# GpSimd's port-using instructions wait for the VectorE instruction one ahead of the port-using one planned before them

## The chip, the cores and the metric

One core of one Trainium2 chip. The metric is device time in microseconds of the one launch, as a median of runs: 1325.54 us for the kernel before (three runs, 1324.97 to 1326.35).

## The reference, cut to what matters

The input is 2 x 4096 tokens of 192 values. Three stages follow each other; nothing crosses from one token to another except in the first.

```
w   = softmax(weight, taps)                       # 8 heads x 7 taps
y0  = sum_k w[h,k] * x[s-6+k]                     # causal convolution, 7 taps
y1  = (sigmoid(y0 @ w_gate) * (y0 @ w_val)) @ w_out          # 192 -> 1536 -> 192
h   = y1 @ w_in                                              # 192 -> 2048
P   = a0 + a1 h + a2 h^2 + a3 h^3
Q   = 1 + |b0||h| + |b1| h^2
out = (P / (Q + 1e-6)) @ w_out2                              # 2048 -> 192
```

Every fp32 matmul operand is split into a high part rounded to fp32r and a low part (what is left), and the products high x high, low x high and high x low are summed.

## The kernel before, in words

The 8192 tokens are 16 tiles of 512 columns, features on the partitions. For each tile there is a convolution (`conv`, with `conv_taps`), a first block (`moe1`) and a second (`moe2`). From the second tile on the convolution runs on GpSimd: seven taps, each a multiplication by a scalar (`tensor_scalar`, L578, into `tmp`) and an addition (`tensor_tensor`, L581, into `ca` or `cb`). The 64 features beyond 128 are done for two tiles at once in `cb`, so every second tile has two such chains of 13 instructions, the others one.

In `moe1` TensorE makes gate and value (lines 662 to 666, five matmuls into a PSUM tile `w`), ScalarE takes the sigmoid (L376), VectorE multiplies by the value from PSUM (L710). The product is split into high (a copy, on ScalarE L376, GpSimd L372 or VectorE L375) and low (a subtraction, on VectorE L387 or GpSimd L385), and TensorE multiplies the parts by `wo_s` into `accb` (L669 to L675). In `moe2` ScalarE and VectorE work the rational function out of `w`: VectorE L777 and L779 read SBUF and PSUM, and L779 is the last reader that gives the tile `w` back to TensorE; L783 and L796 work on 1024 columns with SBUF operands alone. The quotient is split the same way and goes into `accd`. There are four PSUM tiles `w`.

Order is written out by hand. Every operation is put into a `Plan` with an engine (sometimes with a choice of engines), a cost and a priority; `Plan.order` sets the operations in planned time, one engine queue each, and `tc.manual_schedule()` keeps that order on each engine. Each engine then runs its own queue in order, and waits only for the data and buffers that an instruction needs. VectorE and GpSimd operations that read two tensors from SBUF, or copy from SBUF to SBUF, are marked `lock=True`: the planner holds that they share SBUF ports, and never plans two of them at once (`lock_free`; `FREES` is 0.0, so the next starts where the one before ends). Nothing on the chip keeps to that: the planned order between the two engines is not enforced. In the list there are 623 VectorE operations and 339 GpSimd operations with the mark. VectorE's L710, L777, L779, L731 and L820, with one operand in PSUM, do not have it.

The change touches the last lines of the kernel, the loop that emits the list:

```
    order = plan.order(K["look"], K["switch"])
    with tc.manual_schedule():
        for o in order:
            o.emit()
```

Of the kernel before, what the change touches and what calls it, by code (L numbers as in the profile page):

```python
# [13 lines left out]
ALU = mybir.AluOpType  # L14

TOK = 512

HOP = dict(
    PE=dict(ACT=210.0, DVE=210.0, POOL=210.0, SP=210.0),
    ACT=dict(PE=170.0, DVE=170.0, POOL=170.0, SP=170.0),  # L20
    DVE=dict(PE=170.0, ACT=170.0, POOL=170.0, SP=170.0),
    POOL=dict(PE=170.0, ACT=170.0, DVE=170.0, SP=170.0),
# [262 lines left out]
def conv_gated_rational_kernel(  # L285
# [23 lines left out]
    R = D - 128  # L309
    W = 2 * TOK  # L310
    CW = 512
# [5 lines left out]
    for n in K["tiles"]:  # L317
# [7 lines left out]
        "r": ([128, W], F32R, K["slots"]["r"]),  # L325
        "xa": ([128, TOK + 128], F32, 1),
        "xb": ([128, TOK + 128], F32, 1),
        "ca": ([128, TOK], F32, 1),
        "cb": ([128, TOK], F32, 1),
        "tmp": ([128, TOK], F32, 1),  # L330
        "w": ([128, W], F32, 2) if K["pair"] else ([128, TOK], F32, 4),
# [505 lines left out]
        base = nxt  # L837

    order = plan.order(K["look"], K["switch"])
    with tc.manual_schedule():  # L840
        for o in order:
            o.emit()


# ---- launch: one core; the host transposes x and the result, spreads the small vectors and
# [37 lines left out]
```

## Time and profile before

| | |
|---|---|
| median of 3 runs | 1325.54 us |
| the profiled execution: its time, its span | 1323.14 us, 1321.4 us |
| TensorE (PE) busy | 1279.4 us, 97% |
| VectorE (DVE) busy | 1203.2 us, 91% |
| ScalarE (ACT) busy | 1166.8 us, 88% |
| GpSimd (POOL) busy | 485.9 us, 37% |
| granted TensorE clock, mean | 0.995 |
| chain that ended last | PE 50%, ACT 25%, DVE 20%, issue 5% |

Busy time of VectorE and GpSimd is from an instruction's start to its end and includes time in which it waits inside for a port. The 512-column matmuls start every 0.23 us where nothing holds them, and the profile models their ends. Instructions are named by engine and line; L376 is a helper that makes all of ScalarE's plain activations, L387 one that makes all subtractions.

### The profile page before, as it was taken

What the parts mean: (1) busy time and instruction counts of PE and PEld (TensorE: products, weight loads), DVE (VectorE), ACT (ScalarE), POOL (GpSimd) and SP (SyncE); (2) the same over time, 40 slices, a digit from 0 to 9 for tenths busy, and PEclk for the clock granted to TensorE, in tenths of its full rate; (3) what the DMA queues carried; (4) which work ended last, traced back from release to release, by engine and by line L of the source; (5) the groups of instructions that cost most, each with busy time, mean ns of one, the idle gap of its engine ahead of it and who ended that gap; (6) DMA issues with size and microseconds to landing.
All of it is one profiled execution on the core that took longest, in us unless ns stands there. A gap on an engine that the chain in (4) does not pass through costs nothing.

```text
span 1321.4 us, 15094 instructions
## 1 busy us (share of the span) xinstructions
PE 1279.4 (97%) x5492; PEld 1024.0 (77%) x5492; DVE 1203.2 (91%) x1402; ACT 1166.8 (88%) x1506; POOL 485.9 (37%) x344
## 2 busy tenths in 40 slices
PE   8999999999999999999999999999999999999996
PEld 4777777877877878788777887778787787877874
DVE  6999999999989999899988999899898999989997
ACT  7979998898889988898988999889988989889896
POOL 4291504633082511925038150562416533011112
PEclk9999999999999999999999999999999999999998
DMA  6521000000000000000000000000000000000000
GB/s 198 168 68 33 9 1 13 17 13 9 0 21 9 14 7 13 9 9 21 0 13 17 0 21 0 13 17 13 9 1 13 9 13 0 1 12 1 13 12 13
DMA packets 14314, 27.07 MB, mean 20 GB/s; under 512 B 2080, under 2 KB 5792, under 8 KB 14240
## 3 DMA queue, kind: packets, MB, share of 16 engines
q1 hardware_dynamic: 14240, 26.11, 6.8%
q8 instruction: 43, 0.70, 0.2%
q14 instruction: 31, 0.25, 0.1%
HBM read 19.81 MB, written 6.29 MB: 20 GB/s over the span
## 4 chain that ended last, share of the span: by engine, by line
PE 50%; ACT 25%; DVE 20%; issue 5%; POOL 0%; ACTq 0%; DVEq 0%; POOLq 0%
ACT f L376 14%; PE w L662 6%; PE w L666 6%; PE w L663 6%; PE w L665 6%; PE w L664 6%; DVE f L777 4%; ACT L376 4%; ACT r L376 3%; DVE f L796 3%; DVE f L779 3%; DVE r L387 3%; DVE f L783 3%; PE accd L669 2%; PE accd L670 2%
## 5 line engine op out<-in xcount | busy, mean ns | idle before, releaser
L387 DVE TENSOR_TENSOR r<-f,r 128x1024 fp32r<-128x1024 f32 x221 | 289.3, 1323 | 9.8 <-ACT r L376 5.1
L372 POOL TENSOR_SCALAR r<-f 128x1024 fp32r<-128x1024 f32 x50 | 77.5, 1550 | 556.4 <-PE accb L675 170.9
L376 ACT ACTIVATE f<-w,av 128x512 f32<-128x512 f32 x256 | 195.7, 775 | 56.0 <-PE w L666 50.3
L777 DVE TENSOR_TENSOR f<-f,w 128x512 f32<-128x512 f32 x256 | 172.0, 680 | 48.8 <-ACT f L376 48.3
L376 ACT ACTIVATE r<-f 128x1024 fp32r<-128x1024 f32 x169 | 177.6, 1061 | 18.5 <-DVE f L710 15.2
L779 DVE SCALAR_TENSOR_TENSOR f<-f,av,w 128x512 f32<-128x512 f32 x256 | 187.2, 741 | 6.6 <-ACT f L376 3.2
L796 DVE SCALAR_TENSOR_TENSOR f<-f,av,f 128x1024 f32<-128x1024 f32 x128 | 180.7, 1427 | 6.7 <-ACT f L376 6.4
L376 ACT ACTIVATE f<-w,kv 128x512 f32<-128x512 f32 x256 | 172.3, 688 | 11.5 <-DVE f L777 5.5
L783 DVE SCALAR_TENSOR_TENSOR f<-f,bv 128x1024 f32<-128x1024 f32 x128 | 172.3, 1352 | 0.2 <-ACT f L376 0.2
L376 ACT ACT_TABLE_LOAD x126 | 161.7, 1283 | 2.1
L376 ACT ACTIVATE f<-f,kv 128x1024 f32<-128x1024 f32 x128 | 157.9, 1240 | 0.8
L376 ACT ACTIVATE f<-f 128x1024 f32<-128x1024 f32 (+3 forms) x160 | 151.9, 964 | 0.2
L710 DVE TENSOR_TENSOR f<-f,w 128x512 f32<-128x512 f32 x192 | 130.2, 679 | 20.9 <-ACT f L376 13.0
L581 POOL TENSOR_TENSOR ca<-ca,tmp 128x512 f32<-128x512 f32 x90 | 143.0, 1588 | 7.4
L376 ACT ACTIVATE f<-w 128x512 f32<-128x512 f32 x192 | 114.5, 598 | 25.3 <-PE w L666 23.5
L578 POOL TENSOR_SCALAR tmp<-xa,cw 128x512 f32<-128x512 f32 x90 | 118.0, 1311 | 10.5 <-DVE f L777 1.8
L674 PE MATMUL accd<-r,wo_s 128*128 128x512 f32 x256 | 101.3, 396 | 5.9 <-POOL r L385 3.3
L662 PE MATMUL w<-yha,w_h 128*128 128x512 f32 x256 | 102.0, 399 | 5.1 <-DVE f L779 4.0
L669 PE MATMUL accd<-r,wo_s 128*128 128x512 f32 x256 | 100.9, 394 | 3.6 <-ACT r L376 3.2
L675 PE MATMUL accd<-r,wo_s 128*128 128x512 f32 x256 | 100.4, 392 | 0.0
L670 PE MATMUL accd<-r,wo_s 128*128 128x512 f32 x256 | 100.2, 392 | 0.0
L671 PE MATMUL accd<-r,wo_s 128*128 128x512 f32 x256 | 100.2, 391 | 0.0
(111 smaller groups left out, 3001.2 us busy)
## 6 DMA issues: line engine op xcount, KB each, us to landing
f<-in_wo SPq DMA_DIRECT2D x14, 384.0 KB, 3.7
xa<-in_xt SPq DMA_DIRECT2D x16, 259.0 KB, 2.8
out_dram<-f SPq DMA_DIRECT2D x16, 256.0 KB, 2.0
xb<-in_xt SPq DMA_DIRECT2D x16, 129.5 KB, 2.8
f<-in_w SPq DMA_DIRECT2D x4, 512.0 KB, 4.7
out_dram<-f SPq DMA_DIRECT2D x16, 128.0 KB, 2.3
f<-in_wg SPq DMA_DIRECT2D x4, 256.0 KB, 3.7
f<-in_wv SPq DMA_DIRECT2D x4, 256.0 KB, 4.2
```

Of the source, the lines that this page charges most:

```text
L376: plan.op("ACT", (53 if psum else 95) + n * 0.832 + 93 * ptr, prio, lambda: nc.scalar.activation(out=out(), in_=in_(), func=func, **kw), r ...
L387: dve(prio, n, lambda: nc.vector.tensor_tensor(out=out(), in0=in0(), in1=f(in1()), op=ALU.subtract), rd, wr, lock=lock, alts=alts)
L578: plan.op("POOL", 245 + 0.832 * n, p, lambda xin=xin, sc=sc, d=d: nc.gpsimd.tensor_scalar(T(d)[0:np_, 0:n], xin(), sc(), 0.0, op0=ALU.mult ...
L581: plan.op("POOL", 147 + 2.105 * n, p, lambda d=d: nc.gpsimd.tensor_tensor(out=y(), in0=y(), in1=T(d)[0:np_, 0:n], op=ALU.add), rd=[d, acc] ...
L662: nc.tensor.matmul(o, lhsT=wh.tile[:, c], rhs=ha, start=True, stop=False)
L669: nc.tensor.matmul(a1, lhsT=w[:, 0, :], rhs=h, start=first, stop=False)
L670: nc.tensor.matmul(a1, lhsT=w[:, 2, :], rhs=h, start=False, stop=False)
L710: dve(at("gv", t, p), n, lambda sc=sc, val=val: nc.vector.tensor_tensor(out=sc(), in0=sc(), in1=val(), op=ALU.mult), [(pv, "v"), (s, i)], ...
L777: dve(at("v", t, p), sn, lambda q=q, cut=cut, h=h: nc.vector.tensor_tensor(out=cut(u[q]), in0=cut(u[q]), in1=h(), op=ALU.mult), [ps_, (u[q ...
L779: dve(at("w", t, p), sn, lambda q=q, cut=cut, h=h: nc.vector.scalar_tensor_tensor(out=cut(u[q]), in0=cut(u[q]), scalar=av.tile[:, 1:2], in ...
L783: dve(at("y", t, p), gn, lambda q=q: nc.vector.scalar_tensor_tensor(out=C(ha[q]), in0=C(ha[q]), scalar=bv.tile[:, 0:1], in1=C(ha[q]), op0= ...
L796: dve(at("g", t, p), gn, lambda k=k: nc.vector.scalar_tensor_tensor(out=C(u[k]), in0=C(u[k]), scalar=av.tile[:, 0:1], in1=C(ha[k]), op0=AL ...
```

## The change

While the list is emitted, the kernel now remembers the VectorE instructions in order. Whenever a VectorE operation with the port mark is emitted, the instruction one place ahead of it in VectorE's queue becomes the gate. A GpSimd operation with the mark gets a synchronised dependency on the gate of that moment: it may not start before that VectorE instruction has completed. So GpSimd can start at the earliest when the last port-using VectorE instruction planned before it is about to start. VectorE gets no new wait. Order, costs, buffers and instructions are the same.

```diff
+PORT_BACK = 1
...
     order = plan.order(K["look"], K["switch"])
+    line, gate = [], None
     with tc.manual_schedule():
         for o in order:
-            o.emit()
+            lock = o.opts[o.eng][2] if o.eng in ("DVE", "POOL") else False
+            made = o.emit()
+            made = made.ins if hasattr(made, "ins") else None
+            if o.eng == "DVE":
+                line.append(made)
+                if lock and len(line) > PORT_BACK:
+                    gate = line[-1 - PORT_BACK]
+            if o.eng == "POOL" and lock and gate is not None and made is not None:
+                tc.add_manual_dep(made, gate.name, mybir.DependencyInfo(
+                    mybir.DependencyClass.Sync, mybir.DependencyReason.ANTI), reason="port order")
```

## Rows read from the trace of the kernel before

**Rows 1.** The page: the span, and each engine's busy time and share
```profile
span 1321.4 us, 15094 instructions
PE 1279.4 (97%) x5492; PEld 1024.0 (77%) x5492; DVE 1203.2 (91%) x1402; ACT 1166.8 (88%) x1506; POOL 485.9 (37%) x344
```

**Rows 2.** TensorE's waits: who for whom, us in total, times, longest us
```profile
PE w L662 <- DVE f L779: 20.3, 25, 1.4
```

**Rows 3.** VectorE by line and shape: count, busy us, mean ns, idle before
```profile
L387 DVE TENSOR_TENSOR r<-f,r 128x1024 fp32r<-128x1024 f32 x221 | 289.3, 1323 | 9.8 <-ACT r L376 5.1 <-PE accd L671 4.4
...
L796 DVE SCALAR_TENSOR_TENSOR f<-f,av,f 128x1024 f32<-128x1024 f32 x128 | 180.7, 1427 | 6.7 <-ACT f L376 6.4
L783 DVE SCALAR_TENSOR_TENSOR f<-f,bv 128x1024 f32<-128x1024 f32 x128 | 172.3, 1352 | 0.2 <-ACT f L376 0.2
...
L387 DVE TENSOR_TENSOR xlb<-cb,xhb 64x512 fp32r<-64x512 f32 x32 | 27.9, 873 | 2.4 <-ACT xhb L376 1.8
```

**Rows 4.** Single lines of VectorE and GpSimd: duration ns min/median/max, first and last start
```profile
L387 DVE TENSOR_TENSOR r<-f,r x221: 1205/1218/2316, 31.5 to 1311.3; 128x1024 fp32r<-128x1024 f32 x111
...
L387 DVE TENSOR_TENSOR xlb<-cb,xhb x32: 675/688/1811, 22.1 to 1169.2; 64x512 fp32r<-64x512 f32 x32
...
L796 DVE SCALAR_TENSOR_TENSOR f<-f,av,f x128: 1268/1279/2314, 107.0 to 1308.8; 128x1024 f32<-128x1024 f32 x128
...
L783 DVE SCALAR_TENSOR_TENSOR f<-f,bv x128: 1267/1278/2221, 90.1 to 1299.1; 128x1024 f32<-128x1024 f32 x128
...
L375 DVE CAST r<-f x5: 678/682/2240, 1277.0 to 1304.4; 128x1024 fp32r<-128x1024 f32 x5
...
L578 POOL TENSOR_SCALAR tmp<-xa,cw x90: 692/1545/2605, 19.4 to 1096.8; 128x512 f32<-128x512 f32 x90
```

**Rows 5.** The timeline around 717 us: start, us, engine, instruction, idle before
```profile
717.12 1.29 POOL L581 TENSOR_TENSOR cb<-cb,tmp 128x512 f32<-128x512 f32 x1
...
717.25 2.23 DVE L796 SCALAR_TENSOR_TENSOR f<-f,av,f 128x1024 f32<-128x1024 f32 x1
719.41 1.39 DVE L779 SCALAR_TENSOR_TENSOR f<-f,av,w 128x512 f32<-128x512 f32 x2
...
720.20 0.50 PE L662 MATMUL w<-xha,wg_h 128*128 128x512 f32 x1 [0.75 <-DVE f L779]
```

**Rows 6.** The timeline at 611 and 689 to 697 us, VectorE and GpSimd
```profile
611.92 2.60 POOL L578 TENSOR_SCALAR tmp<-xa,cw 128x512 f32<-128x512 f32 x1
...
611.47 1.43 DVE L783 SCALAR_TENSOR_TENSOR f<-f,bv 128x1024 f32<-128x1024 f32 x1
612.82 1.21 DVE L387 TENSOR_TENSOR r<-f,r 128x1024 fp32r<-128x1024 f32 x1
...
689.07 0.69 DVE L777 TENSOR_TENSOR f<-f,w 128x512 f32<-128x512 f32 x1 [1.65 <-ACT f L376]
...
696.36 2.92 DVE L796 SCALAR_TENSOR_TENSOR f<-f,av,f 128x1024 f32<-128x1024 f32 x2
...
696.47 1.73 POOL L578 TENSOR_SCALAR tmp<-xa,cw 128x512 f32<-128x512 f32 x1
```

**Rows 7.** The timeline of the end, 1288 to 1301 us: GpSimd, VectorE, TensorE
```profile
1288.43 4.46 POOL L385 TENSOR_TENSOR r<-f,r 128x1024 fp32r<-128x1024 f32 x1 [8.12 <-DVE r L375]
...
1291.20 2.24 DVE L375 CAST r<-f 128x1024 fp32r<-128x1024 f32 x1
...
1293.61 2.41 POOL L385 TENSOR_TENSOR r<-f,r 128x1024 fp32r<-128x1024 f32 x1 [0.72 <-DVE r L375]
...
1300.65 0.50 PE L669 MATMUL accd<-r,wo_s 128*128 128x512 f32 x1 [2.70 <-ACT r L376]
```

**Rows 8.** Timeline, GpSimd's copy at 626 us and its consumer; waits as instructions of their own
```profile
626.49 1.80 POOL L372 TENSOR_SCALAR r<-f 128x1024 fp32r<-128x1024 f32 x1 [3.73 <-PE accb L675]
...
630.38 1.22 DVE L387 TENSOR_TENSOR r<-f,r 128x1024 fp32r<-128x1024 f32 x1
...
L372 POOLq EVENT_SEMAPHORE  x48: 17/17/11323, 109.8 to 1256.2; - x48
```

## The prediction

> **What bounds the kernel.** First the page: TensorE is busy 97% of the span, VectorE 91%, ScalarE 88%, GpSimd 37% [rows 1]. TensorE is idle for 1321.4 - 1279.4 = 42.0 us, start and end of the kernel included, so nothing done for VectorE can give more than a part of 42 us. Next TensorE's waits: the largest is L662, the first matmul into a PSUM tile, held by VectorE's L779, the last reader of that tile: 20.3 us in 25 waits [rows 2]. So VectorE being late is what costs TensorE time, but only in 25 places.
>
> Then VectorE by line and shape, beside the same lines' minimum and median. The median is 11 to 13 ns above the minimum and the maximum some 0.9 to 1.1 us above it [rows 4]; the means lie between [rows 3]. Count times (mean - median): 221 x (1323 - 1218) = 23.2 us, 128 x (1427 - 1279) = 18.9, 128 x (1352 - 1278) = 9.5, 32 x (873 - 688) = 5.9, together 57.5 us. The timeline shows what it is: L796 at 717.25 takes 2.23 us instead of 1.28, because GpSimd's addition began at 717.12 and ran to 718.41; the whole second instruction waits [rows 5].
>
> Last, the planner's list laid beside the trace (each engine ran its queue in that order). By my count, 97 of the 111 obstructed VectorE instructions stand ahead of the GpSimd instruction that obstructed them: GpSimd had overtaken the plan. Of 336 marked GpSimd instructions that get a gate, 199 started before the instruction that is now their gate had ended. The addition of 717.12 is one: its gate is the second L779 of the pair that starts at 719.41, which ended at 720.80 [rows 5].
>
> **The change, part by part.** *What is taken away.* Those 97 obstructions, nearly all of the 57.5 us of VectorE time. On the path that sets the end counts only what stands before one of the 25 waits.
>
> (a) Around 717: with the addition held until the pair of L779 is through, L796 runs its 1.28 us and ends at 718.53 and the two L779 follow 0.95 us sooner. TensorE's L662 at 720.20 then waits not 0.75 us but nothing [rows 5]. The same figure returns at 402.4, 561.4, 879.0 and 1037.7: 5 x 0.75 = 3.75 us.
>
> (b) The other waits on L779 hold 20.3 - 3.75 = 16.5 us. They gain between nothing and 16.5 us. Many have another chain in front: before the longest of the steady part VectorE stood 1.65 us for ScalarE at 689.07 [rows 6], and a faster VectorE only waits longer there. I take 3.0 us, near the low end for the sake of that row.
>
> (c) The end. The cast at 1291.20 takes 2.24 us instead of 0.68 behind GpSimd's subtraction of 1288.43, which the list has behind the cast [rows 4, 7]. VectorE's queue from there to the end is the chain that ends last, so up to 1.56 us come free. ScalarE feeds what follows the cast, so I take 1.0 us. The subtraction starts only when the cast is through, at about 1291.9, and needs 2.4 us, so it ends at 1294.3 instead of 1292.89; the matmuls behind it have 2.70 us to spare at 1300.65, where TensorE waits for ScalarE anyway [rows 7].
>
> Together 7.75 us.
>
> *What is added.* A wait per GpSimd instruction, many of them already covered by the one before; where it needs an instruction of its own that takes 17 ns [rows 8], 336 x 17 ns = 5.7 us at most on an engine that is busy 37% [rows 1]. I cost it at nothing; what hides it is GpSimd's idle time.
>
> *What is moved.* GpSimd's instructions start later: the 199 by up to 10 us, most by 0.5 to 5, judged by the end of the gate in the trace. Behind them in its queue stand the rest of the taps and the copies (L372). The taps are due some 40 us later (the split by ScalarE), and the load of the next `xa`, which waits in SP's queue for the last tap, has the same room, as have the stores behind it in that queue. The copies feed VectorE's subtraction and TensorE's L669: the tightest common case is the copy that ends at 628.29, for a subtraction at 630.38, 2.09 us of room [rows 8]. Of the other copies that come 2 us or more ahead of their gate, all but one have more room than that.
>
> *What is given back.* The list itself has GpSimd instructions between two port-using VectorE instructions that ran back to back in the trace: 46 places. Held to its order, GpSimd can get in there, and the second VectorE instruction waits. The trace has both outcomes: at 696.47 GpSimd got in and the two L796 took 2.92 us instead of 2.48; at 611.92 it waited 1.9 us through both L783 and L387, and neither lost by it [rows 6]. Ends: nothing, and 46 x 0.9 us (between one multiplication of 0.69 and an addition of 1.29) = 41 us of VectorE time. Half is 20 us. Of the 57.5 us taken away 7.75 are on the path, 13%; the same share of 20 us is 2.6 us.
>
> [...]
>
> Sum: 7.75 - 2.6 = 5.1 us less. The profiled execution took 1323.14 us, the median of the runs is 2.4 us higher, 1325.54. So 1318.0 against the profiled execution, and **1320.4 us** as a median.
>
> **The rivals.** *Collisions are only exchanged.* GpSimd is admitted at most of the 46 places and collides anew elsewhere; VectorE loses as much as before, only where the list says. For it: VectorE and GpSimd need the ports for the same total time. Against it: the five places of (a) and the cast of (c), 4.75 us, do not depend on that. Net 0 to 2.6 us less: about 1324.5 us.
>
> *A new wait of VectorE for GpSimd's copies (slower).* Held behind back-to-back VectorE instructions, a chain of taps runs late, and the copy behind it in GpSimd's queue is late for the subtraction in VectorE's. It decides from 2.09 us of lateness on [rows 8]. In the chain before that copy a single instruction is already held 1.9 us [rows 6]. Price: four tiles have that copy; with 3 us of VectorE each and a TensorE wait to match, 12 us, less the gain of 7.75 and with the 2.6 given back: 6.9 us more, 1332 us. Against it: GpSimd stands idle 3.73 us just before that copy, which takes up that much [rows 8].
>
> *More of (b).* With VectorE ahead by up to 4 us a tile, half of the waits on L779 go: 8.25 instead of 3.0, so 10.4 us less, 1315 us. Against it: the row at 689.07 [rows 6].
>
> *The gate does nothing*, since earlier waits on the same engine already imply it. That holds for 137 of the 336; for 199 the trace shows a start before the gate's end. I count it to the first rival.
>
> **How the numbers follow.** A measurement of this kernel tells about 0.2% (2.65 us) from no change. Forecast 0.40, more of (b) 0.15, exchange 0.25, new wait 0.20. The forecast's own range, with (b) from 0 to 6 and the return from 0 to 5.3, is 1314.8 to 1326.0; a little of it is within 0.2%, and a little of the exchange falls on either side. Faster 0.54, same 0.24, slower 0.22. The range for 8 in 10 reaches into both rivals: 1310 to 1331.
>
> **What would show it.** Right: mean of L796 near 1.30 us and L783 near 1.30 (from 1427 and 1352 ns), L387 near 1.27; the waits of L662 on L779 down from 20.3 to about 13 us, with none of 0.75 at the place of 720.20; the cast of the end at 0.68 us; GpSimd's taps each starting after their gate, its copies waiting for VectorE instead of TensorE. Wrong: VectorE's obstructed time still near 57 us, now on the second of two neighbours (exchange); a row in VectorE's waits on GpSimd's L372, which does not exist now (new wait); TensorE's idle time unchanged although VectorE's means fall, which would say that ScalarE's chain, not VectorE, sets these waits.

## The result, and the profile after

The changed kernel takes 1307.61 us (median of four runs, 1307.09 to 1307.99) against 1325.26 us for the kernel before on the same chip: a ratio of 0.9868, 95% interval 0.9851 to 0.9885, 17.6 us less. Forecast were 1320.4 us, 1310 to 1331. The direction held, the size did not. In the changed kernel every line number up to the planner's call is 2 higher: L781 is the L779 of before, L798 the L796, L785 the L783, L389 the L387, L664 the L662.

The page of the changed kernel, its span and the busy times:

```profile
span 1305.3 us, 15243 instructions
...
PE 1274.0 (98%) x5492; PEld 1025.4 (79%) x5492; DVE 1172.7 (90%) x1402; ACT 1165.2 (89%) x1506; POOL 501.9 (38%) x344
```

VectorE is busy 30.5 us less than in [rows 1] with the same 1402 instructions, ScalarE is nearly unchanged, TensorE is idle 31.3 us instead of 42.0. Of the 16.1 us of the span that is 10.7; the other 5.4 us went out of TensorE's busy time, with the same 5492 matmuls. The 149 instructions more are waits that stand on GpSimd's queue as instructions of their own.

VectorE by line and shape (count, busy us, mean ns, idle before) in the changed kernel, the four groups of [rows 3]:

```profile
L389 DVE TENSOR_TENSOR r<-f,r 128x1024 fp32r<-128x1024 f32 x221 | 283.3, 1296 | 10.0 <-ACT r L378 5.6 <-PE accd L673 4.2
...
L798 DVE SCALAR_TENSOR_TENSOR f<-f,av,f 128x1024 f32<-128x1024 f32 x128 | 175.0, 1382 | 6.7 <-ACT f L378 6.2
L785 DVE SCALAR_TENSOR_TENSOR f<-f,bv 128x1024 f32<-128x1024 f32 x128 | 163.9, 1286 | 0.1
...
L389 DVE TENSOR_TENSOR xlb<-cb,xhb 64x512 fp32r<-64x512 f32 x32 | 22.3, 697 | 2.5 <-ACT xhb L378 1.8
```

Count times (mean - the median of [rows 4]), the measure of the prediction: 17.2 + 13.2 + 1.0 + 0.3 = 31.7 us lost inside VectorE's instructions at the ports, where it was 57.5. "Ports" is the planner's word. What the trace of before shows is this: all 111 VectorE instructions that took over 0.14 us more than the median of their line and shape ran beside a marked GpSimd instruction, and of the 736 of the five lines with an operand in PSUM, 320 of which ran beside one too, none took more than 0.013 us over its median. Laid beside the planner's list, 2 obstructed VectorE instructions were overtaken (97 before) and 58 stand behind the GpSimd instruction that obstructs them, as the list has it (14 before). So overtaking is gone, and about half of what it cost VectorE came back as foreseen collisions: by a wider count, over all obstructed instructions and not the four groups alone, some 60 us of overtaking became 1.5, and some 6 us of foreseen collisions became 35.

TensorE's waits (who for whom, us in total, times, longest):

```profile
PE w L664 <- DVE f L781: 12.8, 16, 2.0
PE accd L676 <- POOL r L387: 3.9, 1, 3.9
```

The wait for VectorE's release of `w` is down from 20.3 us in 25 to 12.8 us in 16 [rows 2]. GpSimd's waits show the gate at work:

```profile
POOL r L374 <- PE accb L673: 90.7, 7, 30.2
POOL r L374 <- DVE f L779: 82.0, 8, 19.4
POOL r L374 <- DVE f L712: 78.0, 5, 16.5
...
POOL tmp L580 <- DVE f L781: 8.5, 13, 1.0
```

The copies (L374) read what L798 wrote, and yet wait 78.0 us for L712: that is the gate, and before there was no such row. Their longest row of before, 170.9 us in 15 waits for `accb`, is down to 90.7 in 7. No row of VectorE's waits names a copy of GpSimd, so the new wait that the third rival feared did not come.

The timeline at the place of [rows 5], VectorE, GpSimd and TensorE:

```profile
709.46 1.36 DVE L779 TENSOR_TENSOR f<-f,w 128x512 f32<-128x512 f32 x2 [0.63 <-ACT f L378]
710.74 1.28 DVE L798 SCALAR_TENSOR_TENSOR f<-f,av,f 128x1024 f32<-128x1024 f32 x1
711.93 1.40 DVE L781 SCALAR_TENSOR_TENSOR f<-f,av,w 128x512 f32<-128x512 f32 x2
...
710.97 2.21 POOL L583 TENSOR_TENSOR cb<-cb,tmp 128x512 f32<-128x512 f32 x1 [0.79 <-DVE f L779]
...
715.17 1.30 POOL L583 TENSOR_TENSOR cb<-cb,tmp 128x512 f32<-128x512 f32 x1
...
712.77 0.46 PE L664 MATMUL w<-xha,wg_h 128*128 128x512 f32 x1
```

By the order of GpSimd's queue the addition that began at 717.12 before is the one at 715.17 here: it starts behind both L781 (711.93 and 1.40 us), so it no longer stands ahead of L798, which takes 1.28 instead of 2.23, and TensorE has no wait. The addition at 710.97 is an earlier one, of 714.10 before. It waits 0.79 us for its gate, starts 0.23 us behind L798 and stands the rest of L798 inside its own 2.21 us (the one at 715.17 takes 1.30): here the collision costs GpSimd, not VectorE.

**Where the 16.1 us of the span went.** TensorE's queue is the same 5492 matmuls in both traces, so the start of the same matmul can be compared. Against before it comes 1.9 us earlier at 160 us, 2.1 at 329, 11.1 at 1058, 13.2 at 1254, and the last one 16.1. From 329 to 1058 us that is 1.8 to 2.1 us for each pair of tiles, and 0.91 of it comes at the one matmul of [rows 5] and its sisters (402, 561, 720, 879, 1038 us), 0.28 at the one that stood 1.35 us (692 us and sisters), the rest mostly in steps of 0.05 to 0.25.

Split by matmul, the 25 waits of [rows 2] are not the whole path. Between 90 and 1254 us, 8.3 us were gained at those 25 matmuls, of which 4.5 at the five places of 717 us and its sisters, and 5.0 us at matmuls that have no row in those 25 waits. One of these, before:

```profile
962.54 0.39 PE L671 MATMUL accb<-r,wo_s 128*128 128x512 f32 x1
962.98 0.50 PE L662 MATMUL w<-yha,w_h 128*128 128x512 f32 x1
963.32 0.39 PE L663 MATMUL w<-yha,w_l 128*128 128x512 f32 x1
963.55 0.40 PE L664 MATMUL w<-yla,w_h 128*128 128x512 f32 x1
```

and the same in the changed kernel:

```profile
953.21 0.39 PE L673 MATMUL accb<-r,wo_s 128*128 128x512 f32 x1
953.44 0.39 PE L664 MATMUL w<-yha,w_h 128*128 128x512 f32 x1
953.66 0.39 PE L665 MATMUL w<-yha,w_l 128*128 128x512 f32 x1
```

Before, L662 starts 0.44 us behind its forerunner and the next one 0.34 us behind that, where 0.23 is usual: 0.33 us lost, and the view shows no wait, since the end that it gives the forerunner (962.93) leaves 0.05 us idle. Nine such stops for the same L779, with the start behind them (the next matmul came 0.33 to 0.34 us later and not 0.23), make 2.4 of the 5.0 us.

The end, VectorE and GpSimd:

```profile
1277.51 0.68 DVE L377 CAST r<-f 128x1024 fp32r<-128x1024 f32 x1
1278.11 0.73 DVE L781 SCALAR_TENSOR_TENSOR f<-f,av,w 128x512 f32<-128x512 f32 x1
...
1277.73 5.02 POOL L387 TENSOR_TENSOR r<-f,r 128x1024 fp32r<-128x1024 f32 x2 [11.10 <-DVE f L779]
...
1280.46 0.80 PE L676 MATMUL accd<-r,wo_s 128*128 128x512 f32 x1 [3.94 <-POOL r L387]
```

The cast is at 0.68 us instead of 2.24 [rows 7]. The subtraction starts 0.22 us behind the cast's start and not behind its end: its gate is the L779 ahead of the cast. TensorE waits 3.94 us for the subtraction (2.77 before), and as foreseen it does not matter: the wait of 2.70 us for ScalarE behind it is gone. Around these waits the granted clock of TensorE was 0.5 instead of 1.0 for 6.8 us in both traces, from 1301.7 us before and from 1278.5 us here.

### The profile page after: what moved, and what is told of

The parts are those of the page before. It is cut to its first block, busy times and chain, and to the rows that moved or that the text cites. A ratio compares the mean times of both kernels' runs of the same rounds, so it can differ in the third digit from the quotient of the medians.

```text
span 1305.3 us, 15243 instructions
## 1 busy us (share of the span) xinstructions
PE 1274.0 (98%) x5492; PEld 1025.4 (79%) x5492; DVE 1172.7 (90%) x1402; ACT 1165.2 (89%) x1506; POOL 501.9 (38%) x344
## 4 chain that ended last, share of the span: by engine, by line
PE 62%; ACT 23%; DVE 11%; issue 3%; POOL 0%; ACTq 0%; DVEq 0%; POOLq 0%
ACT f L378 14%; PE w L664 7%; PE w L668 7%; PE w L665 7%; PE w L666 7%; PE w L667 7%; ACT L378 3%; PE accd L676 3%; PE accd L671 3%; PE accd L673 3%; PE accd L672 3%; PE accd L677 3%; ACT r L378 3%; DVE f L779 2%; PE accb L671 2%
## 5 line engine op out<-in xcount | busy, mean ns | idle before, releaser
L389 DVE TENSOR_TENSOR r<-f,r 128x1024 fp32r<-128x1024 f32 x221 | 283.3, 1296 | 10.0 <-ACT r L378 5.6
L374 POOL TENSOR_SCALAR r<-f 128x1024 fp32r<-128x1024 f32 x50 | 81.1, 1623 | 500.5 <-PE accb L673 90.7
L378 ACT ACTIVATE f<-w,av 128x512 f32<-128x512 f32 x256 | 195.7, 775 | 51.8 <-PE w L668 46.4
L779 DVE TENSOR_TENSOR f<-f,w 128x512 f32<-128x512 f32 x256 | 172.1, 681 | 58.6 <-ACT f L378 58.1
L781 DVE SCALAR_TENSOR_TENSOR f<-f,av,w 128x512 f32<-128x512 f32 x256 | 187.4, 743 | 6.6 <-ACT f L378 3.2
L798 DVE SCALAR_TENSOR_TENSOR f<-f,av,f 128x1024 f32<-128x1024 f32 x128 | 175.0, 1382 | 6.7 <-ACT f L378 6.2
L785 DVE SCALAR_TENSOR_TENSOR f<-f,bv 128x1024 f32<-128x1024 f32 x128 | 163.9, 1286 | 0.1
L583 POOL TENSOR_TENSOR ca<-ca,tmp 128x512 f32<-128x512 f32 x90 | 150.8, 1675 | 18.0 <-DVE f L779 5.3
L712 DVE TENSOR_TENSOR f<-f,w 128x512 f32<-128x512 f32 x192 | 130.2, 679 | 24.0 <-ACT f L378 15.8
L664 PE MATMUL w<-yha,w_h 128*128 128x512 f32 x256 | 101.4, 396 | 2.9 <-DVE f L781 2.3
```

The costliest lines, as they stand in the source:

```text
L378: plan.op("ACT", (53 if psum else 95) + n * 0.832 + 93 * ptr, prio, lambda: nc.scalar.activation(out=out(), in_=in_(), func=func, **kw), r ...
L389: dve(prio, n, lambda: nc.vector.tensor_tensor(out=out(), in0=in0(), in1=f(in1()), op=ALU.subtract), rd, wr, lock=lock, alts=alts)
L583: plan.op("POOL", 147 + 2.105 * n, p, lambda d=d: nc.gpsimd.tensor_tensor(out=y(), in0=y(), in1=T(d)[0:np_, 0:n], op=ALU.add), rd=[d, acc] ...
L664: nc.tensor.matmul(o, lhsT=wh.tile[:, c], rhs=ha, start=True, stop=False)
L779: dve(at("v", t, p), sn, lambda q=q, cut=cut, h=h: nc.vector.tensor_tensor(out=cut(u[q]), in0=cut(u[q]), in1=h(), op=ALU.mult), [ps_, (u[q ...
L781: dve(at("w", t, p), sn, lambda q=q, cut=cut, h=h: nc.vector.scalar_tensor_tensor(out=cut(u[q]), in0=cut(u[q]), scalar=av.tile[:, 1:2], in ...
```

## The experiments

Two theories were put up. **A, amount**: the time follows what VectorE loses at the ports; 30 us less made 17 us, 0.54 us for each. **B, place**: a collision that the list foresaw costs nothing, since the planner puts it where VectorE would stand anyway; one that the list did not foresee costs TensorE time. "Lost" below is the sum over the four groups as above; for e8 VectorE's waits for GpSimd are added.

| kernel | lost at the ports, us | median, us | ratio to before, 95% |
|---|---|---|---|
| before | 57.5 | 1325.3 | |
| changed | 31.7 | 1307.6 | 0.9851 to 0.9885 |
| e1, gate on the instruction itself | 33.8 | 1308.8 | 0.986 to 0.9889 |
| e2, gate two ahead | 62.0 | 1322.6 | 0.9973 to 0.9992 |
| e3, taps alone gated | 47.5 | 1315.1 | 0.9907 to 0.994 |
| e4, copies and subtractions alone | 51.8 | 1317.6 | 0.9926 to 0.9956 |
| e5, gate eight ahead | 61.2 | 1326.5 | 0.9995 to 1.0014 |
| e6, gate, taps left out | 0.7 | 1306.8 | 0.9838 to 0.9868 |
| e7, the three subtractions alone | 60.8 | 1323.6 | 0.9975 to 0.9993 |
| e8, both directions | 62.8 | 1309.8 | 0.9865 to 0.9898 |
| e9, taps of the second chain alone | 53.2 | 1320.6 | 0.9951 to 0.9977 |
| e10, no gate, taps left out | 9.0 | 1314.4 | 0.9902 to 0.9931 |
| e11, gate from 40 us on | 32.3 | 1308.4 | 0.9856 to 0.9889 |

**How far ahead.**

```diff
-PORT_BACK = 1
+PORT_BACK = 0
```

> The gate is the port-using VectorE instruction itself, so GpSimd starts only after it has ended. Theory A (the time follows what VectorE loses inside its instructions at the ports; 30 us less of that gave 17 us): GpSimd no longer gets in between two neighbouring VectorE instructions, so VectorE loses less than the 37 us of the changed kernel, 20 to 30 us, and the time falls to 1301 to 1305 us. Theory B (what counts is the place: a collision that the planner foresaw costs nothing, one that it did not foresee costs TensorE time): the foreseen collisions go, which cost nothing, and GpSimd is later than planned, so 1306 to 1311 us.

1308.78 us. The loss did not fall as A's sentence supposed (33.8 us, not 20 to 30): GpSimd starts later and meets the next VectorE instruction instead, as the list has it (75 of 76 obstructed instructions). The time fits B's band, and A's slope too.

```diff
-PORT_BACK = 1
+PORT_BACK = 2
```

> The gate is two VectorE instructions ahead, so GpSimd may overtake by one instruction (0.6 to 1.3 us). Theory A: it is in the ports when the port-using instruction arrives, VectorE loses 50 us or more, time 1316 to 1322 us. Theory B: only overtakings by more than one instruction matter for the drift, most of the gain of 17 us stays if the collisions fall elsewhere; 1310 to 1316 us. Both: slower than with one ahead.

1322.64 us, just above A's band; B's guess of how much stays was wrong. Overtaking by a single instruction is enough to lose nearly everything: 90 obstructed instructions were overtaken, as against 97 without a gate. Yet VectorE loses more here than before (62.0 against 57.5 us) and the kernel is 2.6 us faster, which A does not give. By the wider count its overtaking is some 54 us and its foreseen collisions some 19.

```diff
-PORT_BACK = 1
+PORT_BACK = 8
```

> The gate lies eight VectorE instructions ahead, so the same waits are there but hold hardly any order. If waits as such, or GpSimd being a little later, did something to the time, it shows here; theories A and B both say no: VectorE loses 65 to 72 us as before, 1323 to 1327 us.

1326.51 us, no difference that the interval shows. The waits themselves cost nothing and bring nothing; order does.

**Which instructions.**

```diff
-if o.eng == "POOL" and lock and gate is not None ...
+if o.eng == "POOL" and lock and getattr(o.prio, "cls", "") in ("cv", "cb") and gate is not None ...
```

> Only the convolution's taps are gated; the copies and subtractions of the split are free as before. Both theories: the places at 93, 402, 561, 720, 879 and 1038 us are obstructed by taps, so the gain up to 1100 us (12 us) stays; the end (2.9 us) and the stretch from 1120 us on (1 to 2 us) are lost. 1311 to 1313 us.

```diff
+... getattr(o.prio, "cls", "") not in ("cv", "cb") and ...
```

> Only the copies and subtractions of the split are gated; the taps are free. Both theories: the gain of the end (2.9 us) and 1 to 3 us of the rest: 1320 to 1322 us. If the copies' wait costs TensorE something that the taps' gain hides, it shows here as a time at or above 1325 us.

1315.1 and 1317.55 us: gains of 10.1 and 7.7 us, together 17.8, where both at once give 17.6. So the two parts add up. Both bands were missed: the 50 copies and 3 subtractions are worth more than the ledger gave them, the 154 multiplications and 132 additions less.

The two traces also split by place. Between 90 and 1254 us, with the taps alone gated, TensorE gains 9.2 us at the 25 matmuls of [rows 2] and loses 1.2 at the others. With the copies and subtractions alone gated it gains nothing at those 25, whose row stays as it was,

```profile
PE w L664 <- DVE f L781: 20.1, 25, 1.4
```

and 4.5 us at the others.

```diff
+... getattr(o.prio, "cls", "") == "lo2" and ...
```

> Only GpSimd's three subtractions at the end are gated. The step (c) of the prediction: the cast takes 0.68 us instead of 2.24. If the 2.9 us that the end gained are the cast's, 1322 to 1323 us; if the end gains because VectorE arrives with the copies of the last tile out of its way, under 1 us: 1324 to 1326 us.

1323.6 us, a ratio of 0.9984. Between the two bands: the three subtractions are worth 2.1 us by the ratio (0.9 to 3.3 by its interval), and whether that is the whole 2.9 us of the end stays open. In the trace the end, from 1254 us on, gains 2.4 us, but the granted clock of TensorE was 0.5 for 3.4 us there instead of 6.8 (mean of the run 0.997, of before 0.995), so the cast's own share can't be told.

```diff
+... getattr(o.prio, "cls", "") == "cb" and ...
```

> Only the taps of the second chain (into cb, every other tile) are gated. The addition of 717 us and its four sisters are such taps. By the ledger of the changed kernel (0.91 us at each of the five places, about 2 us before 100 us): 1318 to 1321 us. If the five places are not caused by these taps, 1323 us or more.

1320.55 us, inside the band. In its trace TensorE's matmul comes 0.91, 0.90, 0.91 and 0.90 us earlier at the places of 402, 561, 720 and 879 us, and only 0.32 us at 1038 us, where the obstructing tap is one of the first chain; with all taps gated (e3) that place gains 0.90 too. So step (a) is shown, place by place.

**Amount or place.** The next leave out the second to seventh tap, with the gate (e6) and without any (e10), or keep the list in both directions (e8).

```diff
+            if o.eng == "POOL" and any(b.kind == "tmp" for b in o.bufs):
+                continue
             made = o.emit()
```

> The changed kernel with the second to seventh tap of tiles 1 to 15 left out of the convolution (so its result is the first tap alone there); the list and the gate are as they were. The collisions with those taps go, foreseen ones too: VectorE should lose under 12 us instead of 40. Theory A (0.54 us of time for each us that VectorE loses): some 28 us less lost, 1290 to 1295 us. Theory B (foreseen collisions cost nothing): 1303 to 1308 us.

1306.8 us. VectorE loses 31 us less than in the changed kernel, and the time falls by 0.8 us, which the intervals do not tell from nothing. Theory A wanted 1290 to 1295. Where the 31 us went is in VectorE's waits of that run:

```profile
DVE f L779 <- ACT f L378: 73.2, 86, 2.1
DVE f L712 <- ACT f L378: 22.0, 28, 2.1
DVE f L733 <- ACT f L378: 17.1, 14, 1.6
```

and the same rows of the changed kernel:

```profile
DVE f L779 <- ACT f L378: 58.1, 71, 1.7
DVE f L712 <- ACT f L378: 15.8, 15, 2.0
DVE f L733 <- ACT f L378: 7.8, 14, 1.4
```

112.3 us against 81.7: 30.6 us more of waiting for ScalarE. The foreseen collisions stood in time that VectorE would have spent waiting for ScalarE.

```diff
+            if o.eng == "POOL" and lock and made is not None:
+                last = made
+            if o.eng == "DVE" and lock and last is not None and made is not None:
+                tc.add_manual_dep(made, last.name, mybir.DependencyInfo(
+                    mybir.DependencyClass.Sync, mybir.DependencyReason.ANTI), reason="port order")
```

> The gate as in the change, and VectorE's port-using instructions also wait for the last marked GpSimd instruction planned before them to have completed, so the list is kept in both directions. Theory A: VectorE stands outside its instructions instead of inside, for as long or longer (GpSimd late now holds VectorE): 1312 to 1325 us. Theory B, in the form that the planned order itself is worth something: 1300 to 1307 us.

1309.8 us, between the two bands (B up to 1307, A from 1312). What decides is how much VectorE loses here. VectorE's waits in e8:

```profile
DVE r L389 <- POOL tmp L580: 12.4, 21, 0.7
DVE r L389 <- POOL ca L583: 12.3, 14, 1.2
DVE f L798 <- POOL ca L583: 9.1, 9, 1.2
...
DVE f L798 <- POOL tmp L580: 6.2, 12, 0.6
```

and its instructions:

```profile
L389 DVE TENSOR_TENSOR r<-f,r 128x1024 fp32r<-128x1024 f32 x221 | 267.1, 1221 | 37.0 <-POOL tmp L580 12.4 <-POOL ca L583 12.3 <-PE accd L673 3.6
L798 DVE SCALAR_TENSOR_TENSOR f<-f,av,f 128x1024 f32<-128x1024 f32 x128 | 164.0, 1292 | 22.6 <-POOL ca L583 9.1 <-POOL tmp L580 6.2 <-ACT f L378 5.6
```

All rows on GpSimd together are 59.9 us in 84 waits, and 2.9 us are still lost inside the four groups: 62.8 us. The waits are those of all VectorE instructions, so the fair measure of before is the wider count, some 66 us, and not the 57.5 of the four groups. VectorE loses nearly as much and the kernel is 15 us faster than before; only where it loses it is different.

```diff
-            if o.eng == "POOL" and lock and gate is not None and made is not None:
+            if False:
```

on top of the edit of e6:

> The kernel before with the second to seventh tap of tiles 1 to 15 left out, and no gate at all: only GpSimd's copies and subtractions are left, and they overtake freely. VectorE should lose 15 to 20 us of its 70. If any 30 us of relief bring the gain (amount), this one has 50 us and comes out at 1306 to 1308 us, as the run with the same taps left out and the gate kept. If overtaking itself costs (theory B), the copies' overtaking still costs the 4 to 8 us that gating them alone gave back: 1311 to 1315 us.

```profile
L389 DVE TENSOR_TENSOR r<-f,r 128x1024 fp32r<-128x1024 f32 x221 | 268.0, 1227 | 9.9 <-ACT r L378 5.4 <-PE accd L673 4.3
L798 DVE SCALAR_TENSOR_TENSOR f<-f,av,f 128x1024 f32<-128x1024 f32 x128 | 165.8, 1311 | 7.2 <-ACT f L378 6.8
L785 DVE SCALAR_TENSOR_TENSOR f<-f,bv 128x1024 f32<-128x1024 f32 x128 | 165.7, 1301 | 0.1
```

1314.4 us, inside B's band. By the means of these rows VectorE loses 2.0 + 4.1 + 2.9 = 9.0 us (15 to 20 were expected). That is a seventh of what it loses in e8, and the kernel is 4.6 us slower than e8 and 7.6 us slower than e6, from which it differs by the gate alone, which there holds the copies, the subtractions and the 22 first taps: their overtaking costs 7.6 us, as much as gating copies and subtractions brought in e4 (7.7). Amount is refuted as the cause; it went with the time in e1, e3, e4 and e5 because gating some instructions removes overtaking and amount together. That the time can't fall below some 1306 us, whatever VectorE gains, would explain e6, but neither e8 nor e10. Nor is there one price for overtaking: by the wider count e3 keeps some 24 overtakings, mostly by copies, and is 7.5 us slower than the changed kernel, while e4 keeps some 92, by taps, and is 9.9 us slower.

```diff
+... lock and o.start > 40000.0 and gate is not None ...
```

> The change with the gate left off for GpSimd instructions planned before 40 us. In the changed kernel one wait of TensorE at 31.6 us is 1.2 us longer than before. If that is the gate's doing, 1306.0 to 1307.0 us; if not, the changed kernel's 1307.6 within 0.5 us.

1308.44 us (1307.09 to 1309.8): no gain, and just outside both bands. In its trace the longer wait at 31.6 us is gone, so the gate makes it, but it is not worth anything; and no version that computes all taps is better than the change.

## Why the prediction was right in direction and wrong in size

- **What is taken away** was right: 57.5 us of obstructions were found in the means, nearly all ascribed to overtaking, and overtaking fell to 2 instructions.
- **(a)** 3.75 us forecast, 4.5 measured (5 x 0.91): the wait of 0.75 us, and 0.16 us by which the matmul came later than its wait alone tells. e9 and e3 show the cause.
- **(b)** 3.0 us forecast, 3.8 measured at the other 20 of the 25 waits. The row at 689.07, for the sake of which it was put low, was a fair sample: there the gain was 0.28 us.
- **The path** is the step that failed: "On the path that sets the end counts only what stands before one of the 25 waits." On those 25 the prediction was nearly right, and its own sign for them came true: 20.3 us of waits were to fall to about 13 and fell to 12.8. But 5.0 us of the gain up to 1254 us came at matmuls outside them, half of it in stops too short to be listed, and the prediction put that at nothing. e4 shows whose they are: gating the copies and subtractions alone brings 4.5 us there and nothing at the 25. The prediction looked at the copies only as something that might be late.
- **The return** failed as well: 2.6 us, as "the same share of 20 us". The collisions that came back are more than supposed (about 30 us of VectorE time by the wider count), and with the taps among them removed the kernel gains 0.8 us. The 5.3 us at the far end of its range, 13% of 41 us, no run shows either. For the same reason L796's mean came to 1.38 us and not to the 1.30 that was named as a sign. Taking one share of the path for both kinds was the error: overtaking costs more than the 13% (16.1 us of span for some 59 us, 27%), the foreseen kind almost nothing.
- **(c)** 1.0 us forecast, 2.9 at the end with all gates; 2.1 (0.9 to 3.3) in time from the subtractions alone (e7). Its reading of the gate was wrong: the subtraction does not wait for the cast's end, it starts just behind the cast, and the cast takes 0.68 us all the same.
- **Sum** of the span: (a) 4.5, (b) 3.8, outside the 25 waits 5.0, the end 2.9, less 0.1 before 90 us, make 16.1 us; the return stands inside these. Against the forecast of 5.1 that is 0.8 + 0.8 + 5.0 + 1.9 + 2.6 - 0.1 = 11.0 us more.
- The **rivals**: exchange is refuted as a whole (amount was exchanged by half, time was not); the new wait of VectorE for copies did not appear. "More of (b)" came nearest in time with 1315 us, but not by its mechanism: the waits on L779 outside (a) gave 3.8 us and not 8.25.

Why overtaking costs more than a foreseen collision is shown in its effect, not in each place: VectorE's relief from foreseen collisions turned into waits for ScalarE (e6), its relief from overtaking in part into time. That GpSimd overtakes just when VectorE is behind the list, and so delays the engine that is late already, is the reading that fits; it was not tried by itself.

## What to carry to other kernels

Here a mean that lay clear above the median of the same instruction (L796 before: 1427 against 1279 ns) was the sign that another engine obstructed it; before pricing such a thing, ask of each obstruction whether the schedule foresaw it. A table of waits lists only what is long enough to be seen: here a third of the gain came from stops outside the row that looked like the path, half of them too short for the table, and laying the starts of the same matmuls of two traces side by side shows them. Where an order between two engines was planned and nothing keeps it, let the less loaded engine wait for the instruction just ahead of the one it must not pass: here that is worth 1.3%, and one place more of slack in it loses most of that. Time lost on a busy engine is not a currency: 62.8 us in foreseen places cost less than 9.0 us in unforeseen ones.

## What the runs showed of the hardware that was not expected

When GpSimd started a marked instruction while VectorE ran one of its own and had the next one right behind it, it was sometimes let in between (the second VectorE instruction took longer) and sometimes not: in the trace of before 31 to 35 times and 20 to 22 times, depending on how close a neighbour must be to count. At 696.47 it started 0.11 us after the first VectorE instruction and got in; at 611.92, 0.45 us after, it did not [rows 6]. Additions got in every time (10 in the trace of before, 15 in that of the changed kernel); those passed over were multiplications, copies and one subtraction, while other multiplications and copies got in. What decides stays open. A wait as an instruction of its own took 17 ns on GpSimd's queue in the median [rows 8], and eight-ahead gates, with 120 such instructions more than before (15214 against 15094), changed nothing that can be measured (ratio 0.9995 to 1.0014).
